# Attention and a two-layer network: the quarter sums of the second weight made by GpSimd from float32 instead of by sign matmuls

## The chip, the cores and the metric

The kernel runs on one core of a Trainium2 chip. The time of a run is the device time of the program in microseconds (us), and lower is better. The engines are named as the profile names them: PE (TensorE, matmuls; PEld are its weight loads), DVE (VectorE), ACT (ScalarE), POOL (GpSimd) and SP (SyncE, which issues most transfers). Each engine takes its instructions in the order in which they were written into its queue, and waits when an operand is not there yet.

## The reference

The input `x` has 8 batches of 8 heads, 512 rows of 64; `state` has 32 rows for each head. Both directions of attention are computed, put together to 544 rows of 512 for each batch, and sent through a normalised network of two layers with ReLU and a residual. The weights are stored in 64-bit floating point.

```python
scale = 1.0 / np.sqrt(D)
scores = scale * np.matmul(x, state.transpose(0, 1, 3, 2))
scores = scores - scores.max(-1, keepdims=True)
a = np.exp(scores)
a /= a.sum(-1, keepdims=True) + 1e-09
xread = np.matmul(a, state)
...
sread = np.matmul(a2, x)
...
xn = (x - mu) / np.sqrt(var + 1e-06) * g_ln
ch = np.maximum(xn @ w_ch1, 0.0) @ w_ch2
return (x + ch).astype(np.float32)
```

`w_ch1` is 512 x 2048 and `w_ch2` 2048 x 512.

## The kernel before

**Precision and tiles.** Every large product is done in float16 halves: a float32 value is split into a high half (`ACTIVATE` with Copy on ACT) and a low half (`SCALAR_TENSOR_TENSOR` on DVE: value times scale, minus the high half), and three matmuls (high x high, high x low, low x high, `TERMS`) replace one. `split` (L663) is that pair. The hidden 2048 columns are worked in four units (`U` = 4) of 512.

**Weights.** `weights1(u)` (L680) and `weights2(u)` (L714) fetch the unit u of the two weights. The 64-bit words land as pairs of 32-bit integers in two landing places (`raws`), each 128 x 2048 words for half of a unit; `words` (L646) builds float32 values out of them, which lie in the first landing place afterwards (`t`). Then come a bound on the size (`sum_of_squares`, `scales`) and the splits into `w1c[u]` and `w2h[u]`. The landing places are parts of buffers that are needed otherwise later (`extra(k)`, whose tile is called `sums`, and `unit(k)`, `narrow(k)`, `wide(k)`, `odd`, called `raw`), so where a unit lands decides from when on it can be fetched and until when it can stay.

**Batch 0** is computed unit by unit while the weights arrive: `state_products` (L750) makes `matrix`, `first_products` (L793) the hidden block with its halves `hid` (the low half of which GpSimd makes, `hid<-strip,hid` 128x512), `second_product` (L813) multiplies with `w2h[u]`, 12 matmuls of 512 columns for each 128 rows (L817); the partial results are added up by transfers that GpSimd issues (`xr<-part`), the last unit's by DVE (`xr<-acc,of_unit,xr`).

**Batches 1 to 7 and the state rows** use Strassen and Winograd's scheme with seven products for the second layer: `products(b)` (L874), with `first` (L901, `half<-ea,matrix`) for the hidden block, `multiply` (L959) for the products and `together` (L968) for the result. A unit of the second weight is seen as four quarters b11, b12, b21, b22 of 128 x 512 values (256 rows by 256 columns), and the scheme needs three or four sums of them besides: b22 - b12, b12 - b11, b22 - b12 + b11, and b21 less the third.

**The sums before** are made by PE from the float16 halves. `sums_of_weights(u)` (L843) multiplies the halves with an identity or its negative (`signs`, L318) and accumulates: 32 matmuls for a unit (L849), 128 in all, each 256 columns; every sum is copied into its high half by ACT (`sums<-acc`, `w2h<-acc`, 128x256) and its low half is made by DVE (`TENSOR_TENSOR sums<-acc,sums`, 128x256), 32 of each in all. The second difference replaces the quarter b12 in `w2h[u]`, so plain second products of batch 0 with that unit have to be done by then; the others lie in `sums16`.

**Attention of batch 1** is made while batch 0 ends. Its softmax in the `ts` layout goes DVE (`dA`, `mA`, `RECIPROCAL mA`), GpSimd (`ts<-ts,mA` 128x1024), DVE (`STREAM_TRANSPOSE ef`), ACT and DVE (`ea`).

**What sets the order.** `PLAN` (L38) is a table written out by hand: items "stream:steps", read in turn by `issue` (L190), which writes each step's instructions into the queues. So the order on each engine is the order of that table, and streams are interleaved as it says. A last stream holds `WARM` (L162) filler matmuls, `half<-ones`, 128x512, whose result nobody reads; they stand between the matmuls of the first 55 us.

Of the kernel before, what the change touches and what calls it, by code (L numbers as in the profile page):

```python
# [9 lines left out]
F16 = mybir.dt.float16  # L10
# [191 lines left out]
def moe_attention(ctx: ExitStack, tc: tile.TileContext, x, state, g_ln, w1, w2, out):  # L202
# [116 lines left out]
    for i in range(2):  # L319
        nc.vector.tensor_scalar(signs[:, i], idf, 1.0 - 2.0 * i, None, ALU.mult)  # L320
# [761 lines left out]
```

## Time and profile before

| | |
|---|---|
| median of 3 runs | 639.22 us (638.99 to 640.02) |
| profiled execution: its own time | 638.32 us |
| its span (first to last instruction) | 636.5 us |
| mean granted TensorE clock | 0.997 |
| ACT, busy | 375.7 us (59%) |
| filler matmuls `half<-ones` | 111, from 1.1 to 54.7 us |
| sign matmuls L849 | 128, from 110.0 to 153.6 us |

The profile's page lists busy time for each engine, the chain of work that ended last, and groups of like instructions. The trace behind it can be asked for a stretch of the span, a line, a tile, or a timeline. In a timeline row the first number is the start in us, the second the length, then engine, line, operation, output `<-` inputs, shape and count; in brackets stands how long the engine had been idle and what ended that. In a row of groups, count, total us and mean ns stand behind the shape, then the idle time before. Rows of instructions that directly follow one another and are alike are drawn together in a timeline, with one length for all of them.

### The profile page before, as it was taken

To read this page: it belongs to the slowest core of one execution; us is meant where nothing else is said; L and a number is where in the kernel's file an instruction comes from. 1 tells how busy PE (TensorE), PEld (TensorE's weight loads), DVE (VectorE), ACT (ScalarE), POOL (GpSimd) and SP (SyncE) were. 2 spreads that over 40 slices of the span, in tenths; PEclk is the share of its full clock that TensorE was granted. 3 is DMA by queue.
4 is the path that set the end of the run, shared out by engine and by line. 5 is a ranking of instruction groups with operands and counts; after the bars stand their busy time and mean duration, and the time that the engine had idled before them with its cause. 6 is when DMAs were issued, how large, how long until landed. Compare 5 with 4: busy or idle time off the path is not lost.

```text
span 636.5 us, 16845 instructions
## 1 busy us (share of the span) xinstructions
PE 621.7 (98%) x7010; PEld 493.6 (78%) x7010; DVE 491.2 (77%) x1105; ACT 375.7 (59%) x686; POOL 228.5 (36%) x189
## 2 busy tenths in 40 slices
PE   9998999999999999999999999999999999999995
PEld 4464555768888888888888888788878888988884
DVE  5999999758795888798778886887487888555543
ACT  5998987768364846584465555755663545343332
POOL 0123435311451335333533453154323544323231
PEclk9999999999999999999999999999999999999998
DMA  8995666330515242515350335043405024201001
GB/s 292 408 267 204 110 158 130 75 79 11 138 34 144 82 77 58 131 26 122 72 150 10 71 91 147 21 78 101 115 2 115 2 44 127 69 1 35 34 34 34
DMA packets 85356, 62.04 MB, mean 97 GB/s; under 512 B 64608, under 2 KB 77408, under 8 KB 84832
## 3 DMA queue, kind: packets, MB, share of 16 engines
q1 hardware_dynamic: 83008, 57.00, 33.4%
q0 software_dynamic: 864, 3.15, 2.7%
q8 instruction: 55, 0.90, 0.6%
q10 hardware_dynamic: 1408, 0.82, 0.4%
q14 instruction: 21, 0.17, 0.1%
HBM read 28.05 MB, written 9.44 MB: 59 GB/s over the span
## 4 chain that ended last, share of the span: by engine, by line
PE 82%; ACT 6%; DVE 6%; DMA 3%; issue 1%; POOL 1%; SPq 0%; ACTq 0%; POOLq 0%; DVEq 0%
PE acc L959 41%; PE half L901 22%; PE half L911 3%; PE banks L757 3%; PE acc L817 3%; PE acc L849 2%; ACT sums L187 1%; DVE raw L187 1%; PE half L187 1%; ACT raw L187 1%; PE banks L594 1%; PE acc L803 1%; PE banks L476 1%; DMA ek<-ek 1%; DMA xr<-part 1%
## 5 line engine op out<-in xcount | busy, mean ns | idle before, releaser
L959 PEld LDWEIGHTS <-xs 128*128 128x128 f16 x2520 | 243.7, 98 | 37.6 <-issue 7.7
L187 POOL TENSOR_TENSOR xs<-rs,xs 128x512 f16<-128x512 f32 x120 | 145.4, 1221 | 270.0 <-ACT xs L187 187.9
L959 PE MATMUL acc<-w2h,xs 128*128 128x256 f16 x1440 | 181.7, 273 | 0.0
L901 PE MATMUL half<-ea,matrix 128*128 128x256 f16 x1344 | 160.8, 273 | 0.1
L901 PEld LDWEIGHTS <-matrix 128*128 128x128 f16 x1344 | 129.9, 98 | 19.6 <-issue 3.0
L959 PE MATMUL acc<-sums,xs 128*128 128x256 f16 x1080 | 140.1, 273 | 0.0
L187 DVE SCALAR_TENSOR_TENSOR rs<-half,rs 128x256 f32<-128x256 f32 x224 | 90.2, 418 | 48.1 <-ACT rs L187 26.7
L187 ACT ACTIVATE xs<-rs 128x512 f16<-128x512 f32 (+1 forms) x128 | 77.2, 618 | 48.6 <-DVE rs L187 46.1
L187 ACT ACTIVATE xs<-half 128x256 f16<-128x256 f32 (+1 forms) x112 | 54.0, 486 | 81.7 <-PE half L901 39.8
L187 DVE SCALAR_TENSOR_TENSOR xs<-half,xs 128x256 f16<-128x256 f32 (+1 forms) x112 | 60.6, 550 | 18.8 <-ACT xs L187 16.3
L187 POOL TENSOR_TENSOR ts<-ts,mA 128x1024 f32<-128x1024 f32 (+1 forms) x16 | 31.6, 1974 | 62.0 <-DVE mA L187 55.5
L187 ACT ACTIVATE rs<-half 128x256 f32<-128x256 f32 x56 | 21.3, 380 | 39.6 <-PE half L901 36.6
L187 DVE SCALAR_TENSOR_TENSOR matrix<-banks,hs,matrix 128x1024 f16<-128x1024 f32 x28 | 35.8, 1279 | 11.2 <-ACT matrix L187 11.0
L817 PE MATMUL acc<-w2h,hid 128*128 128x512 f16 x192 | 43.4, 379 | 0.5 <-DVE of_weights L187 0.5
L187 DVE TENSOR_TENSOR strip<-acc,strip 128x256 f32<-128x256 f32 (+1 forms) x60 | 32.9, 549 | 13.4 <-PE acc L959 10.5
L187 ACT ACTIVATE matrix<-banks,hs 128x1024 f16<-128x1024 f32 x28 | 31.0, 1108 | 12.9 <-PE banks L757 12.7
L187 POOL TENSOR_TENSOR hid<-strip,hid 128x512 f16<-128x512 f32 x16 | 25.4, 1600 | 30.0 <-ACT hid L187 29.5
L817 PEld LDWEIGHTS <-hid 128*128 128x128 f16 x192 | 18.2, 98 | 21.6 <-issue 1.5
L187 PE MATMUL half<-ones 128*128 128x512 bf16 x111 | 27.8, 397 | 1.1 <-DVE ones L316 1.1
L187 DVE SCALAR_TENSOR_TENSOR xr<-strip,of_second,xr 128x512 f32<-128x512 f32 x28 | 26.6, 957 | 0.0
L187 DVE SCALAR_TENSOR_TENSOR x<-x_f,x_s,x 128x512 f16<-128x512 f32 x32 | 24.5, 801 | 1.2 <-ACT x L187 1.0
L187 ACT ACTIVATE x<-x_f,x_s 128x512 f16<-128x512 f32 x32 | 22.0, 713 | 4.8 <-DVE x_s L327 4.6
(156 smaller groups left out, 751.1 us busy)
## 6 DMA issues: line engine op xcount, KB each, us to landing
raw<-in_moe_w_ch_dram SPq DMA_DIRECT2D x10, 1024.0 KB, 8.8
out_dram<-xr SPq DMA_DIRECT2D x16, 512.0 KB, 3.0
x_f<-in_x_dram SPq DMA_DIRECT2D x14, 512.0 KB, 5.3
sums<-in_moe_w_ch_dram SPq DMA_DIRECT2D x6, 1024.0 KB, 7.6
ek<-ea SPq DMA_DIRECT2D x56, 64.0 KB, 2.0
ek<-ek SPq DMA_DIRECT2D x7, 512.0 KB, 4.3
xr<-part POOLq DMA_DIRECT2D x6, 512.0 KB, 5.4
s_r<-in_state_dram SPq DMA_DIRECT2D x28, 64.0 KB, 3.5
```

The lines of the kernel that those rows point to most:

```text
L187: return lambda: f(*map(now, args), **{k: now(v) for k, v in kw.items()})
L476: nc.tensor.matmul(o[32 * j:32 * j + 32], lhsT=state_of(b, sT, g, j, a), rhs=xT[:, 2 * j + g].rearrange("p c t -> p (c t)"), start=a == 0, ...
L594: nc.tensor.matmul(px[:, c, D * h:D * h + D], lhsT=ek[:, h % 2, h // 2, (2 * t + c) * P:(2 * t + c + 1) * P], rhs=sk[:, h], start=True, st ...
L757: nc.tensor.matmul(ps[g][32 * j:32 * j + 32], lhsT=state_of(b, sT, g, j, i)[r], rhs=w[r, k, j], start=n == 0, stop=n == 2, skip_group_chec ...
L803: nc.tensor.matmul(o[:, 256 * f:256 * f + 256], lhsT=m[:, g, i, P * (q + f):P * (q + f) + P], rhs=ea[:, s, k, g], start=f == 0 and g == 0 ...
L817: nc.tensor.matmul(po, lhsT=hid[:, i, q, c * P:(c + 1) * P], rhs=w[:, j, q], start=first and q == 0 and n == 0, stop=last and q == 3 and n ...
L849: nc.tensor.matmul(o, lhsT=signs[:, k // 2], rhs=v[k], start=start and k == 0, stop=k == 3, skip_group_check=True)
L901: nc.tensor.matmul(ps[:, 256 * q:256 * q + 256], lhsT=m[:, h, i, P * (2 * k + q):P * (2 * k + q) + P], rhs=ea[:, 0, j, h, 256 * g:256 * g ...
L911: nc.tensor.matmul(ps[:, 256 * q:256 * q + 256].rearrange("p (t n) -> p t n", t=2), lhsT=w[:, i, j, fs], rhs=xsT[:, :, x, j], start=q == 0 ...
L959: nc.tensor.matmul(po[o], lhsT=y[:, n, i, o] if o < 2 else x[:, o - 2, n, i], rhs=v[j], start=u == 0 and n == 0 and k == 0 and o in (2, 1, ...
```

## The change

The sums are made before the split and not after it. When the float32 values of a unit of the second weight have been split into `w2h[u]`, GpSimd takes differences of their quarters in place in the landing place (`w2f[u]`), four `TENSOR_TENSOR` of 128x512 float32 for a unit, 16 in all; then each of the four results is split, as any weight is, by one ACT and one DVE instruction of 128x512: 16 of each. `signs` and the 128 matmuls, 32 copies and 32 subtractions are gone. The results of the splits stay in parts of the `extra` buffers that are free then (`strassen_homes`). As the values of a unit must stay until the sums are made, the last unit of the first weight lands in `unit(2)` and the last of the second in `unit(3)`. `WARM` goes from 111 to 131. The streams of the sums for units 0, 1 and 2 come directly behind unit 2's, so that the numbers of the streams in the table change, and the table is a new one throughout.

```diff
-WARM = 111
+WARM = 131
...
-    signs = main.tile([P, 2, P], F16, name="signs")
-    for i in range(2):
-        nc.vector.tensor_scalar(signs[:, i], idf, 1.0 - 2.0 * i, None, ALU.mult)
...
         raws = ((extra(0), extra(1)), (narrow(2, "raw"), wide(2, "raw")), (extra(1), odd("raw")),
-                (extra(2), odd("raw")))[u]
+                (unit(2, "raw"), odd("raw")))[u]
...
         raws = ((extra(2), odd("raw")), (narrow(3, "raw"), wide(3, "raw")), (extra(0), wide(3, "raw")),
-                (unit(2, "raw"), odd("raw")))[u]
-        t = raws[0]
+                (unit(3, "raw"), odd("raw")))[u]
+        t = w2f[u] = raws[0]
...
-    sums16 = sums.bitcast(F16).rearrange("p (u k i n e) -> p u k i n e", u=U, k=3, i=2, n=2)
+    def quarters(t):
+        v = t.rearrange("p (k n e) -> p k n e", k=2, n=2)
+        return [[v[:, k, :, 256 * i:256 * i + 256] for i in range(2)] for k in range(2)]
+
+    def strassen_homes():
+        (a21, a22), (a11, a12) = quarters(extra(2))
+        (c21, c22), (c11, c12) = quarters(extra(0))
+        e = [extra(1)[:, 512 * k:512 * k + 512].rearrange("p (n e) -> p n e", n=2) for k in range(4)]
+        return [[v.bitcast(F16).rearrange("p n (i e) -> p n i e", i=2) for v in vs]
+                for vs in ((a12, a22, a11), (e[0], e[1], e[2]), (c12, c22, c11), (e[3], a21, c21))]
+    sums16 = strassen_homes()
 
     def sums_of_weights(u):
 
-        w = w2h[u].rearrange("p i (k n) e -> p i n k e", n=2)
...
-                yield do(subtract_all, *[v for d, a, b, p in todo for v in (p, *a, *b)])
-                for d, a, b, p in todo:
-                    yield do(nc.scalar.activation, d[0], p, AF.Copy)
-                    yield do(nc.vector.tensor_tensor, d[1], p, d[0], ALU.subtract)
+
+        (b21, b22), (b11, b12) = quarters(w2f[u])
+        s = of_weights[:, U + u, 0:1]
+        w = w2h[u].rearrange("p i (k n) e -> p n i k e", n=2)[:, :, :, 1, 256:512]
+        DIFF = nc.gpsimd.tensor_tensor
+        yield do(DIFF, b22, b22, b12, ALU.subtract)
+        yield do(DIFF, b12, b12, b11, ALU.subtract)
+        yield do(DIFF, b11, b22, b11, ALU.add)
+        yield do(DIFF, b21, b21, b11, ALU.subtract)
+        for o, v in ((w, b12), (sums16[u][0], b22), (sums16[u][1], b11), (sums16[u][2], b21)):
+            yield from split(o[:, :, 0], o[:, :, 1], v, s)
...
-    streams += [common_scale(), attention(1), state_products(1), *map(sums_of_weights, range(U))]
+        if u == 2:
+            streams += map(sums_of_weights, (0, 1, 2))
+    streams += [common_scale(), attention(1), state_products(1), sums_of_weights(3)]
```

Where instructions stand now is seen in the engines' queues. First, seven of the 16 new splits on DVE stand among the last weights of batch 0. This is a piece of DVE's new queue (`sums<-sums,of_weights`, `sums<-raw,of_weights,sums` and `w2h<-...` with 128x2x256 are the new splits; those of 128x1024 split the weights themselves):

```order
L185 SCALAR_TENSOR_TENSOR w2h<-sums,of_weights,w2h 128x2x256
...
L185 SCALAR_TENSOR_TENSOR sums<-sums,of_weights 128x2x256
L185 SCALAR_TENSOR_TENSOR sums<-sums,gx,acc 128x512 x4
L185 SCALAR_TENSOR_TENSOR w1c<-sums,of_weights,w1c 128x1024 x2
L185 SCALAR_TENSOR_TENSOR w2h<-sums,of_weights,w2h 128x1024
L185 TENSOR_REDUCE mB<-banks 128x2
L321 TENSOR_SCALAR mB<-mB,es 128x1 x2
L185 SCALAR_TENSOR_TENSOR matrix<-acc,matrix 128x512 x2
L185 SCALAR_TENSOR_TENSOR sums<-raw,of_weights,sums 128x2x256 x3
L185 SCALAR_TENSOR_TENSOR w2h<-raw,of_weights,w2h 128x2x256
L185 SCALAR_TENSOR_TENSOR sums<-sums,of_weights 128x2x256
```

All seven stand ahead of the next place, DVE's queue around batch 1's RECIPROCAL, which releases `ts` on GpSimd. Before:

```order
L187 RECIPROCAL mA<-mA 128x32
L187 TENSOR_TENSOR w2h<-acc,w2h 128x256
L187 TENSOR_TENSOR sums<-acc,sums 128x256
L187 STREAM_TRANSPOSE ef<-ts 128x1024
L187 TENSOR_TENSOR w2h<-acc,w2h 128x256
L327 TENSOR_SCALAR of_unit<-rf_1087,uoq 128x1 x4
L187 SCALAR_TENSOR_TENSOR ea<-ef,ea 128x1024
L187 TENSOR_TENSOR w2h<-acc,w2h 128x256 x2
L187 SCALAR_TENSOR_TENSOR matrix<-banks,hs,matrix 128x2x512
```

and now:

```order
L185 RECIPROCAL mA<-mA 128x32
L185 TENSOR_SCALAR ux<-x_i 128x1
L321 TENSOR_SCALAR hs<-uoq,r 128x1 x4
L185 TENSOR_SCALAR of_second<-uo 128x1
L185 STREAM_TRANSPOSE ef<-ts 128x1024
L185 SCALAR_TENSOR_TENSOR matrix<-banks,hs,matrix 128x2x512
L185 SCALAR_TENSOR_TENSOR ea<-ef,ea 128x1024
L185 SCALAR_TENSOR_TENSOR w2h<-sums,of_weights,w2h 128x2x256
L185 SCALAR_TENSOR_TENSOR sums<-sums,of_weights 128x2x256
L185 SCALAR_TENSOR_TENSOR matrix<-banks,hs,matrix 128x2x512
```

The subtractions between `RECIPROCAL` and `matrix` are gone; `hs` has moved to behind the RECIPROCAL, and `of_unit` to ahead of it; new splits follow `ea`.

The third place is GpSimd's queue from the hidden lows of unit 2 (the first `hid` x4) to the first hidden block of batch 1 (`xs<-rs,xs`). Before:

```order
L187 TENSOR_TENSOR hid<-strip,hid 128x2x256 x4
L187 DMA xr<-part 128x1024
L187 TENSOR_TENSOR ts<-ts,mA 128x1024
L187 DMA xr<-part 128x1024
L187 TENSOR_TENSOR ts<-ts,mA 128x1024
L187 TENSOR_TENSOR hid<-strip,hid 128x2x256 x4
L187 TENSOR_TENSOR xs<-rs,xs 128x4x128 x5
```

and now, the differences being `sums<-sums` and `raw<-raw`:

```order
L185 TENSOR_TENSOR hid<-strip,hid 128x2x256 x4
L185 DMA xr<-part 128x1024
L185 TENSOR_TENSOR sums<-sums 128x2x256
L185 TENSOR_TENSOR ts<-ts,mA 128x1024
L185 DMA xr<-part 128x1024
L185 TENSOR_TENSOR raw<-raw 128x2x256
L185 TENSOR_TENSOR ts<-ts,mA 128x1024
L185 TENSOR_TENSOR hid<-strip,hid 128x2x256 x2
L185 TENSOR_TENSOR sums<-sums 128x2x256
L185 TENSOR_TENSOR hid<-strip,hid 128x2x256 x2
L185 TENSOR_TENSOR raw<-raw 128x2x256 x2
L185 TENSOR_TENSOR xs<-rs,xs 128x4x128
```

Twelve of the 16 differences stand ahead of the last unit's `hid` (two of them are shown here, ten further up), and four behind. On PE, the first hidden block of batch 1 (24 matmuls of `first`) now stands behind 12 matmuls of the last unit's second product, 24 state products and 12 more of the second product, counted from that unit's first second product on; before, one block of 12 second products stood there. Behind it stand no sign matmuls (88 before), 24 second products of batch 0 (36 before) and 24 state products fewer than before.

More of the change, by code (lines that the diff above doesn't have):

```diff
@@ L637, in statistics @@
         yield columns(len(rows_of), rf, rs, isst, SB, ALU.mult, ALU.mult)
-    w1c, w2h = [None] * U, [None] * U
+    w1c, w2h, w2f = [None] * U, [None] * U, [None] * U
     is1 = Later(lambda: tiny("is1", U))
@@ L839, in second_products_by_unit @@
                 yield from store_batch(0, t)
-    sums16 = sums.bitcast(F16).rearrange("p (u k i n e) -> p u k i n e", u=U, k=3, i=2, n=2)
-    def sums_of_weights(u):
-        w = w2h[u].rearrange("p i (k n) e -> p i n k e", n=2)
-        def subtract(start, o, *v):
-            for k in range(4):
-                nc.tensor.matmul(o, lhsT=signs[:, k // 2], rhs=v[k], start=start and k == 0, stop=k == 3,
-                                 skip_group_check=True)
-        for n in range(2):
-            ps = [accumulator() for _ in range(2)]
-            (b21, b22), (b11, b12) = ([[w[:, i, n, k, 256 * x:256 * x + 256] for i in range(2)] for x in range(2)]
-                                      for k in range(2))
-            t3, t2, n4 = ([sums16[:, u, k, i, n] for i in range(2)] for k in range(3))
-            o = [v[:, 256 * x:256 * x + 256] for v in ps for x in range(2)]
-            for pairs in (((t3, b22, b12), (b12, b12, b11)), ((t2, b22, b12),), ((n4, b21, t2),)):
-                first = len(o)
-                def subtract_all(*v, first=first):
-                    for k in range(len(v) // 5):
-                        subtract(first != 1 and k == 0, *v[5 * k:5 * k + 5])
-                todo = [(d, a, b, o.pop(0)) for d, a, b in pairs]
-                yield do(subtract_all, *[v for d, a, b, p in todo for v in (p, *a, *b)])
-                for d, a, b, p in todo:
-                    yield do(nc.scalar.activation, d[0], p, AF.Copy)
-                    yield do(nc.vector.tensor_tensor, d[1], p, d[0], ALU.subtract)
@@ L956, in multiply @@
                                 q, e = ((n, 0), None, (n + 2, 0), None, None, (n + 2, 256), (n, 256))[o] or (None, None)
-                                v = [w[:, j, q, e:e + 256] if q is not None else wt[:, {3: 0, 4: 1, 1: 2}[o], j, n] for j in range(2)]
+                                v = [w[:, j, q, e:e + 256] if q is not None else wt[{3: 0, 4: 1, 1: 2}[o]][:, n, j] for j in range(2)]
                                 for k, (i, j) in enumerate(TERMS):
@@ L962, in strassen_products @@
                     for ops in ((2, 0, 1), (4,), (3, 5), (6,)):
-                        yield do(lambda po, *a, ops=ops: multiply(ops, [v() for v in po], *a), po, x, y, w2h[u], sums16[:, u])
+                        yield do(lambda po, *a, ops=ops: multiply(ops, [v() for v in po], *a), po, x, y, w2h[u], sums16[u])
                 yield strassen_hidden()
```

242 rows, old and new, of the table PLAN are left out of this document.

## The prediction

> **What bounds the kernel now.** I began with the page's header and its first part, which say which engine is full, and then cut the span into stretches, because a share of the whole span hides where another engine rules.
>
> ```profile
> span 636.5 us, 16845 instructions
> PE 621.7 (98%) x7010; PEld 493.6 (78%) x7010; DVE 491.2 (77%) x1105; ACT 375.7 (59%) x686; POOL 228.5 (36%) x189
> ```
>
> PE is 98% busy over the span. The stretches divide that (start:end, length, then busy time of each engine):
>
> ```profile
> 10.00:58.50 48.50, 43.78 (x608) 24.21 (x606) 47.51 (x90) 46.58 (x73) 11.96 (x7) 1.00 0.89 319
> 58.50:113.00 54.50, 53.84 (x528) 30.10 (x528) 52.88 (x122) 46.13 (x67) 21.30 (x16) 1.00 0.61 135
> 113.00:123.50 10.50, 10.27 (x84) 7.92 (x82) 8.10 (x18) 9.14 (x20) 5.55 (x5) 1.00 0.38 77
> 123.50:300.00 176.50, 176.50 (x2031) 145.80 (x2030) 140.58 (x318) 104.57 (x211) 62.49 (x52) 1.00 0.35 84
> ```
>
> From 10 to 113 us both PE and DVE look full: DVE works 47.51 of 48.5 us and 52.88 of 54.5. Part of PE's busy time there is filler (`WARM`), so fewer matmuls would end nothing sooner in these 103 us; DVE's list does. From 123.5 us on PE has no idle time at all and DVE has a fifth of its time free. So the kernel has two parts: up to the first hidden block of batch 1 (call its start S) DVE and what hangs on it set the pace, and behind S PE does. S and PE's price of one matmul are in PE's timeline:
>
> ```profile
> 119.16 1.91 PE L849 MATMUL acc<-w2h,signs 128*128 128x256 f16 x16 [0.23 <-DVE w2h L187]
> 120.90 2.75 PE L817 MATMUL acc<-w2h,hid 128*128 128x512 f16 x12
> 123.49 1.47 PE L901 MATMUL half<-ea,matrix 128*128 128x256 f16 x12
> ...
> 127.08 0.84 PE L757 MATMUL banks<-w1c,sT 64*32 64x512 f16 x24
> 127.85 0.39 PE L849 MATMUL acc<-w2h,signs 128*128 128x256 f16 x2
> ```
>
> S is 123.49. Durations of matmuls overlap, so a price is taken from one start to the next: 16 sign matmuls in 120.90 - 119.16 = 1.74 us are 0.109 each; 12 second products (L817) in 2.59 are 0.216 each; 24 state products (L757) take 127.85 - 127.08 = 0.77.
>
> **Behind S: what PE saves.** The groups of PE in the stretch from 123.45 to the end:
>
> ```profile
> L757 PE MATMUL banks<-w1c,sT 64*32 64x512 f16 x648 | 22.7, 379 | 0.5 <-DVE matrix L187 0.5
> L849 PE MATMUL acc<-w2h,signs 128*128 128x256 f16 x72 | 10.2, 273 | 0.0
> L817 PE MATMUL acc<-w2h,hid 128*128 128x512 f16 x37 | 8.6, 379 | 0.0
> L849 PE MATMUL acc<-sums,signs 128*128 128x256 f16 x16 | 3.1, 273 | 0.0
> ```
>
> 88 of the 128 sign matmuls stand behind S, and 36 whole second products (the 37th row is one that straddles the cut). In the changed order no sign matmul is left, 24 second products stand behind S, and of the state products one set of 24 has moved ahead of S. PE's work behind S shrinks by 88 x 0.109 + 12 x 0.216 + 0.77 = 9.6 + 2.6 + 0.8 = 13.0 us. PE is full there, so all of it counts: 636.5 - 123.5 = 513.0 us become 500.0. Also gone behind S are the subtractions of the sums on DVE and the copies on ACT; neither engine bounds there, so I price them at nothing; 16 new splits of 128x512 on each take their place, 9 of them behind batch 1's RECIPROCAL (below), and what covers those is the hidden blocks that PE does first. **The span afterwards is S + 500.0**, and the question is where S goes: 13.0 us is the gain if it stays.
>
> **Ahead of S: what DVE gets.** Seven of the 16 new splits stand on DVE ahead of batch 1's RECIPROCAL, which starts the chain to S. Their price is that of a split of the same shape, `x<-x_f,x_s,x`; less the 0.04 us by which one instruction starts ahead of the other's end, 0.70 each.
>
> ```profile
> L187 DVE SCALAR_TENSOR_TENSOR x<-x_f,x_s,x 128x512 f16<-128x512 f32 x8 | 5.8, 742 | 0.0
> ...
> L327 DVE TENSOR_SCALAR hs<-uoq,r 128x1 f32<-128x1 f32 x4 | 0.6, 205 | 0.0
> L327 DVE TENSOR_SCALAR hr<-uoq,r 128x1 f32<-128x1 f32 x4 | 0.6, 204 | 0.0
> ```
>
> ```profile
> 115.11 0.34 DVE L187 RECIPROCAL mA<-mA 128x32 f32<-128x32 f32 x1
> ...
> 117.55 1.25 DVE L187 STREAM_TRANSPOSE ef<-ts 128x1024 f32<-128x1024 f32 x1 [1.49 <-POOL ts L187]
> ...
> 119.03 0.56 DVE L327 TENSOR_SCALAR of_unit<-rf,uoq 128x1 f32<-128x1 f32 x4
> ...
> 122.13 1.28 DVE L187 SCALAR_TENSOR_TENSOR matrix<-banks,hs,matrix 128x1024 f16<-128x1024 f32 x1
> ```
>
> That is +4.9 us. `hs` and `hr`, four each, move behind the RECIPROCAL (-1.2), one set of `of_unit` moves ahead of it (+0.6), one old subtraction is gone (-0.4); the word and split instructions keep their number, their other landing places being worth some 0.0 (I take nothing). Net **+3.9 us**. The old kernel's two sign scalings cost nothing either way: DVE waits for the first input then.
>
> ```profile
> 6.66 0.69 DVE L187 TENSOR_REDUCE most<-x_f 128x1 f32<-128x512 f32 x1 [4.96 <-DMA x_f<-in_x_dram]
> ```
>
> **GpSimd's differences, and what they do to DVE.** Sixteen are added, 128x512 float32 of two inputs, 12 of them ahead of the last unit's hidden lows. The trace has none of the kind. The 128x256 ones (`strip<-strip`) take 0.73, the 128x1024 ones 1.90; the nearest row is `hid`, of the same count of elements, 1.15 when alone. GpSimd is busy a third of the time, so I price its own time at nothing except at the end of the chain. What they do to DVE is the unknown. In the first 113 us some DVE instructions are longer than their like, each under a GpSimd instruction:
>
> ```profile
> L187 POOL TENSOR_TENSOR hid<-strip,hid 128x512 f16<-128x512 f32 x12 | 20.8, 1748 | 21.3 <-ACT hid L187 20.7 <-issue 0.5
> ```
>
> ```profile
> 40.41 2.18 POOL L187 TENSOR_TENSOR hid<-strip,hid 128x512 f16<-128x512 f32 x1 [2.80 <-ACT hid L187]
> 47.36 1.55 POOL L187 TENSOR_TENSOR hid<-strip,hid 128x512 f16<-128x512 f32 x1 [4.78 <-ACT hid L187]
> 53.51 4.30 POOL L187 TENSOR_TENSOR hid<-strip,hid 128x512 f16<-128x512 f32 x2 [4.60 <-ACT hid L187]
> ```
>
> ```profile
> 41.46 1.67 DVE L187 SCALAR_TENSOR_TENSOR ea<-ef,ea 128x512 f16<-128x512 f32 x1
> ...
> 47.94 2.06 DVE L187 SCALAR_TENSOR_TENSOR raw<-raw 128x1024 uint32<-128x1024 uint32 x1
> 49.92 1.27 DVE L187 SCALAR_TENSOR_TENSOR w2h<-sums,of_weights,w2h 128x1024 f16<-128x1024 f32 x1
> ...
> 53.47 1.22 DVE L187 SCALAR_TENSOR_TENSOR sums<-sums 128x1024 uint32<-128x1024 uint32 x1
> 54.72 2.07 DVE L187 SCALAR_TENSOR_TENSOR sums<-raw 128x1024 uint32<-128x1024 uint32 x1
> ...
> 95.63 1.88 DVE L187 SCALAR_TENSOR_TENSOR w2h<-sums,of_weights,w2h 128x1024 f16<-128x1024 f32 x1
> ```
>
> `ea` took 1.67 against 0.74 for a split of its size, two word instructions 2.06 and 2.07 against 1.22, one `w2h` split 1.88 against 1.27: 0.93 + 0.84 + 0.85 + 0.61 = 3.2 us. Twelve `hid` and three `ts` ran on GpSimd in these 103 us, so one of them cost DVE 3.2 / 15 = 0.22 us on average. GpSimd paid too: 1.75 us for a `hid` instead of 1.15. The two ends for 12 new instructions are 0 (none meets a DVE instruction that minds) and 12 x 0.8 = 9.8 us (each stretches one as the four were stretched). I take the average, 12 x 0.22 = **+2.6 us**, since the new instructions fall among the same kind of DVE work.
>
> One rule speaks against the change. The Trainium skill says in "SBUF — State Buffer", section "Who interferes with whom", that DVE's second port pair is also GpSimd's only one, that it is an exclusive lock for whichever came first, and that nothing else among the engines' ports contends. The stretched rows above agree with it in kind, but only 4 of 15 GpSimd instructions cost DVE anything. By the rule at its hardest, with every new difference holding DVE for a `hid`'s 1.15 us, the cost would be 13.8 us in place of 2.6 and the time, as an estimate, about 645.
>
> **The chain to S.** The old chain, with GpSimd's rows beside those of DVE above:
>
> ```profile
> 115.61 1.90 POOL L187 TENSOR_TENSOR ts<-ts,mA 128x1024 f32<-128x1024 f32 x1 [2.12 <-DVE mA L187]
> 117.49 1.15 POOL L187 TENSOR_TENSOR hid<-strip,hid 128x512 f16<-128x512 f32 x1
> ```
>
> The RECIPROCAL ends at 115.45; `ts` runs on GpSimd to 117.51 and the last unit's first `hid` behind it to 118.64. In the old order only one L817 block stood between there and S, and `matrix` (to 123.41) ended last. In the new one GpSimd has the same queue, `ts`, then `hid`, but PE has two second-product blocks of the last unit and a set of state products between that `hid` and S. New RECIPROCAL: 115.45 + 3.9 + 2.6 = 122.0; `ts` 122.1 to 124.0; `hid` to 125.2; PE 0.1 later, then 2 x 2.59 + 0.77 = 5.95: **S = 131.3**. Beside it, DVE's own way (`ef` 1.25, `matrix` 1.28, `ea` 1.28 behind `ts`) ends at 124.0 + 3.8 = 127.8, covered. The 20 more fillers (20 x 0.216 = 4.3 us) stand ahead of the first second product, where PE waits for DVE's splits; nothing is priced for them.
>
> **Sum.** Span 131.3 + 500.0 = 631.3. The profiled run took 638.32, 1.82 beyond its span, so 633.1; the median shown, 639.22, is 0.90 above the profiled run, so the forecast on its footing is **634.0 us**, 0.8% below. A difference of 0.2% (1.3 us) is about what a measurement here can tell from none.
>
> **Rivals.**
> - *The early idle time is used* (0.24). DVE waits some 5 us for its first inputs, and from 113 to 123.5 it is idle 2.4 us, mostly behind `ts`. Work moved into these holes hides the 3.9 us of splits, perhaps part of the stretches. For it: the whole order is new. Against it: the first hole waits for a transfer, which no order fills. S is then 126.5 to 129, the time 629 to 632.
> - *DVE loses nothing* (0.05): S stays near 123.5 to 125 and PE's 13 us come through: 626 to 627.5.
> - *The gain is eaten* (0.09): the time lands within 0.2%, 638 to 640.5, which takes an S of 135.3 to 137.8, 4 to 6.5 us more delay than I summed, as when half of the new differences hit DVE.
> - *GpSimd holds up DVE each time* (0.16), slower. The place is DVE's list from 10 us to the RECIPROCAL, nearly full in both stretches and made of two-input splits and word instructions; the price is the 0.8 us that each of the four stretched rows shows, for 12 differences 9.8 us in place of 2.6. S is then 138.5, the span 638.5, the time 641.2. It decides from 2.6 + 6.5 = 9.1 us on, 0.76 us for each difference. Against it: 11 of 15 GpSimd instructions cost DVE nothing. The lock that the Trainium skill tells of ("SBUF — State Buffer", "Who interferes with whom") would be this mechanism.
>
> **How the numbers follow.** The forecast's case, 632 to 638, holds 0.46 (the range is that of 0.1 to 0.5 us of stretch for a difference, and some early idle time used). Taking the first, third and fourth rivals in, the range is 627 to 641.5, leaving the second rival's edge and the hardest form of the last outside. Faster by over 0.2%: 0.46 + 0.24 + 0.05 = 0.75; within: 0.09; slower: 0.16.
>
> **What would show it.** In the changed kernel the first hidden block should start near 131, and the rest of the span should be 500; if the rest is longer, PE waits behind S, and the first `multiply` is the place. DVE's RECIPROCAL of batch 1 near 122, `ts` right behind, the last unit's first `hid` at 124 and PE idle or filling before it. Between 10 and 113 us DVE's two-input instructions should show some 6 us of stretch instead of 3.2; 12 or more would mean the last rival. The forecast is wrong if the new splits land in idle time, or if PE comes late behind S for want of splits of the sums.

## The result, and the profile after

The changed kernel takes **645.63 us** (median of 4 runs, 644.49 to 646.43) against 639.21 before (four runs): 1.0097 of its time, 95% interval 1.0078 to 1.0115. It is 1% slower; the forecast was 634.0, and the range, 627 to 641.5, does not hold it. The page of the changed kernel begins

```profile
span 644.7 us, 16600 instructions
PE 619.6 (96%) x6902; PEld 485.3 (75%) x6902; DVE 503.7 (78%) x1087; ACT 377.8 (59%) x670; POOL 246.4 (38%) x205
```

PE is busy for 2.1 us less, 619.6 for 621.7, and yet the span is 8.2 us longer. The same stretches as before (engines in the same order; the number behind the counts is the granted clock):

```profile
10.00:58.50 48.50, 43.83 (x586) 23.85 (x585) 47.62 (x81) 48.05 (x70) 7.65 (x6) 1.00 0.92 320
58.50:113.00 54.50, 46.42 (x326) 24.68 (x325) 49.24 (x107) 35.70 (x57) 27.12 (x21) 0.87 0.48 116
```

Up to 58.5 us PE and DVE are as busy as before. From 58.5 to 113 DVE is idle for 5.3 us of 54.5 (1.6 before) and PE for 8.1 (0.7 before), and PE's granted clock fell to 0.87. The chain that the prediction followed, in DVE's, GpSimd's and PE's timelines:

```profile
134.14 0.35 DVE L185 RECIPROCAL mA<-mA 128x32 f32<-128x32 f32 x1
```

```profile
134.64 1.91 POOL L185 TENSOR_TENSOR ts<-ts,mA 128x1024 f32<-128x1024 f32 x1 [0.50 <-DVE hs L321]
136.51 2.27 POOL L185 TENSOR_TENSOR hid<-strip,hid 128x512 f16<-128x512 f32 x2
```

```profile
143.36 2.78 PE L893 MATMUL half<-ea,matrix 128*128 128x256 f16 x24
```

The chain has the shape that was forecast, but it starts 19.0 us later than before (115.45 to 134.49) where 6.5 were summed. S is 143.36, and 644.7 - 143.4 = 501.3 us follow.

Where the 19.0 us are: I took the usual length of each operation and shape on DVE and added up what instructions ahead of the RECIPROCAL took beyond it (over 0.15 us each). The work at usual lengths is 3.1 us more than before, the stretch 14.1 us instead of 3.6, the idle time 13.8 us instead of 9.4; the last 1.0 us is smaller overlap between instructions. Most of the stretched rows, in DVE's timeline:

```profile
56.86 2.11 DVE L185 SCALAR_TENSOR_TENSOR sums<-raw 128x1024 uint32<-128x1024 uint32 x1
58.90 2.17 DVE L185 SCALAR_TENSOR_TENSOR sums<-sums 128x1024 uint32<-128x1024 uint32 x1
...
65.70 2.10 DVE L185 SCALAR_TENSOR_TENSOR sums<-raw 128x1024 uint32<-128x1024 uint32 x1
...
73.47 1.76 DVE L185 SCALAR_TENSOR_TENSOR x<-x_f,x_s,x 128x512 f16<-128x512 f32 x1
...
80.81 1.42 DVE L185 TENSOR_SCALAR raw<-raw 128x1024 uint32<-128x1024 uint32 x1
82.34 2.10 DVE L185 SCALAR_TENSOR_TENSOR sums<-raw 128x1024 uint32<-128x1024 uint32 x1
...
85.10 1.83 DVE L185 SCALAR_TENSOR_TENSOR sh<-s_j,x_s,sh 128x128 f16<-128x128 f32 x1
...
94.57 3.89 DVE L185 SCALAR_TENSOR_TENSOR sums<-sums,of_weights 128x512 f16<-128x512 f32 x1
...
123.76 3.01 DVE L185 SCALAR_TENSOR_TENSOR w1c<-raw,of_weights,w1c 128x1024 f16<-128x1024 f32 x1
```

Usual are 1.22, 1.22, 1.22, 0.74, 0.69, 1.22, 0.34, 0.74 and 1.27. Each of these rows lies beside GpSimd instructions. GpSimd beside the three that lost most:

```profile
83.30 1.05 POOL L185 DMA_DIRECT2D xr<-part  x1
84.09 1.57 POOL L185 TENSOR_TENSOR sums<-sums 128x512 f32<-128x512 f32 x1
85.54 1.24 POOL L185 TENSOR_TENSOR hid<-strip,hid 128x512 f16<-128x512 f32 x1
...
93.40 0.88 POOL L185 DMA_DIRECT2D xr<-part  x1 [6.62 <-ACT part L185]
94.01 1.45 POOL L185 TENSOR_TENSOR hid<-strip,hid 128x512 f16<-128x512 f32 x1
95.13 1.55 POOL L185 TENSOR_TENSOR raw<-raw 128x512 f32<-128x512 f32 x1
96.35 1.55 POOL L185 TENSOR_TENSOR sums<-sums 128x512 f32<-128x512 f32 x1
...
123.48 0.88 POOL L185 DMA_DIRECT2D xr<-part  x1 [0.22 <-issue]
124.10 1.57 POOL L185 TENSOR_TENSOR sums<-sums 128x512 f32<-128x512 f32 x1
```

The split that begins at 94.57 ends 0.56 us after the last of three GpSimd instructions; alone it takes 0.74, so nearly all of its work came behind them. The idle time has rows of its own in the waits of DVE; behind them stand PE's timeline and a piece of the chain that ended last:

```profile
DVE w2h L185 <- ACT w2h L185: 2.8, 2, 2.6
DVE sums L185 <- ACT sums L185: 1.2, 1, 1.2
```

```profile
84.50 1.03 PE L668 MATMUL acc<-sums 128*128 128x128 bf16 x8 [2.15 <-DVE sums L185]
85.47 1.94 PE L696 MATMUL acc<-sums,gm 128*32 128x512 f32 x8
87.34 0.19 PE L349 MATMUL acc<-of_columns,ones 128*128 128x1 bf16 x1
87.38 6.90 PE L811 MATMUL acc<-w2h,hid 128*128 128x512 f16 x24
```

```profile
87.52 4.19 PE acc L811 x12
91.80 0.73 ACT w2h L185
92.55 0.75 DVE w2h L185
```

PE waits for the late DVE and then runs slowly (granted clock 0.50 from 85 to 90 us): 24 second products take 6.9 us where two of the blocks of before, one behind the other, would take 5.3 (2.59 + 2.75). The first 12 of them take 4.19 us in place of 2.59. ACT's split into `w2h` may not overwrite the quarter before those 12 have read it, and DVE waits for ACT.

### The profile page after: what moved, and what is told of

The parts are those of the page before. It is cut to its first block, busy times and chain, and to the rows that moved or that the text cites. A ratio compares the mean times of both kernels' runs of the same rounds, so it can differ in the third digit from the quotient of the medians.

```text
span 644.7 us, 16600 instructions
## 1 busy us (share of the span) xinstructions
PE 619.6 (96%) x6902; PEld 485.3 (75%) x6902; DVE 503.7 (78%) x1087; ACT 377.8 (59%) x670; POOL 246.4 (38%) x205
## 4 chain that ended last, share of the span: by engine, by line
PE 76%; DVE 19%; ACT 3%; issue 1%; DVEq 0%; ACTq 0%
PE acc L951 41%; PE half L893 22%; DVE sums L185 4%; PE half L903 3%; PE banks L751 3%; DVE raw L185 3%; PE acc L811 2%; DVE w1c L185 2%; PE half L185 1%; DVE w2h L185 1%; PE banks L563 1%; PE banks L588 1%; PE banks L470 1%; DVE xs L185 1%; DVE x L185 1%
## 5 line engine op out<-in xcount | busy, mean ns | idle before, releaser
L185 POOL TENSOR_TENSOR xs<-rs,xs 128x512 f16<-128x512 f32 x120 | 143.9, 1211 | 253.8 <-ACT xs L185 169.8
L951 PE MATMUL acc<-sums,xs 128*128 128x256 f16 x1080 | 142.2, 273 | 0.0
L185 ACT ACTIVATE xs<-rs 128x512 f16<-128x512 f32 x128 | 77.1, 618 | 69.3 <-DVE rs L185 62.5
L185 POOL TENSOR_TENSOR ts<-ts,mA 128x1024 f32<-128x1024 f32 (+1 forms) x16 | 30.1, 1880 | 65.2 <-DVE mA L185 62.9
L811 PE MATMUL acc<-w2h,hid 128*128 128x512 f16 x192 | 46.7, 399 | 0.1
L185 DVE SCALAR_TENSOR_TENSOR matrix<-banks,hs,matrix 128x1024 f16<-128x1024 f32 x28 | 35.8, 1279 | 11.9 <-ACT matrix L185 11.9
L185 ACT ACTIVATE matrix<-banks,hs 128x1024 f16<-128x1024 f32 x28 | 31.1, 1111 | 11.8 <-PE banks L751 11.8
L185 PE MATMUL half<-ones 128*128 128x512 bf16 x131 | 33.1, 398 | 1.1 <-DVE part_mean L356 1.1
L185 POOL TENSOR_TENSOR hid<-strip,hid 128x512 f16<-128x512 f32 x16 | 23.6, 1483 | 13.2 <-ACT hid L185 13.2
L185 DVE BATCH_NORM_STATS2 s<-xr 128x6 f32<-128x512 f32 x32 | 21.8, 685 | 5.3 <-ACT xr L185 5.3
```

The costliest lines, as they stand in the source:

```text
L185: return lambda: f(*map(now, args), **{k: now(v) for k, v in kw.items()})
L811: nc.tensor.matmul(po, lhsT=hid[:, i, q, c * P:(c + 1) * P], rhs=w[:, j, q], start=first and q == 0 and n == 0, stop=last and q == 3 and n ...
L951: nc.tensor.matmul(po[o], lhsT=y[:, n, i, o] if o < 2 else x[:, o - 2, n, i], rhs=v[j], start=u == 0 and n == 0 and k == 0 and o in (2, 1, ...
```

## The experiments

"RECIPROCAL" is its end, S the start of the first hidden block, "stretch" and "idle" as above. Ratios are to the kernel before, run beside it; its medians on these six occasions were 639.1 to 639.8 us, so a difference of less than about 1 us between runs of different occasions is not read. The last four columns come from one execution each, and DVE's idle time in the first 20 us alone, ahead of every difference, is 7.0 to 8.6 us in them.

| run | median us | ratio (95%) | RECIPROCAL | S | stretch | idle |
|---|---|---|---|---|---|---|
| before | 639.21 | 1 | 115.5 | 123.5 | 3.6 | 9.4 |
| the change | 645.63 | 1.0097 (1.0078 to 1.0115) | 134.5 | 143.4 | 14.1 | 13.8 |
| 1 tiny differences | 633.51 | 0.9896 (0.9845 to 0.9947) | 122.6 | 131.5 | 5.2 | 10.8 |
| 2 on DVE | 643.71 | 1.0073 (1.0046 to 1.0100) | 130.3 | 139.8 | 6.6 | 9.8 |
| 3 fillers | 644.04 | 1.0081 (1.0051 to 1.0111) | 132.3 | 141.2 | 14.2 | 11.6 |
| 4 unit 0 late | 644.92 | 1.0084 (1.0038 to 1.0129) | 132.5 | 142.8 | 8.4 | 16.9 |
| 5 twice | 647.86 | 1.0132 (1.0103 to 1.0161) | 134.2 | 143.9 | 15.7 | 12.2 |
| 6 halves | 637.56 | 0.9980 (0.9968 to 0.9991) | 127.2 | 136.1 | 10.4 | 10.3 |
| 7 tiny, fillers | 636.23 | 0.9948 (0.9925 to 0.9970) | 125.2 | 134.1 | 5.2 | 13.1 |
| 8 by transfer | 653.61 | 1.0222 (1.0166 to 1.0278) | 140.5 | 149.8 | 6.0 | 27.3 |
| 9 halves, lows too | 640.77 | 1.0020 (1.0002 to 1.0038) | 130.3 | 139.0 | 13.0 | 10.9 |
| 10 quarters | 638.45 | 0.9991 (0.9977 to 1.0005) | 128.9 | 137.8 | 10.3 | 12.1 |
| 11 before, lows in halves | 637.74 | 0.9978 (0.9963 to 0.9994) | 114.4 | 122.4 | 2.3 | 9.4 |
| 12 halves, 111 fillers | 640.38 | 1.0010 (0.9993 to 1.0026) | 129.5 | 138.3 | 9.8 | 12.9 |
| 13 one transfer behind | 644.60 | 1.0082 (1.0057 to 1.0107) | 131.7 | 140.5 | 13.2 | 11.8 |
| 14 same, halves | 637.49 | 0.9974 (0.9961 to 0.9987) | 127.1 | 136.0 | 10.2 | 10.3 |
| 15 both behind | 641.97 | 1.0033 (1.0021 to 1.0044) | 129.5 | 138.3 | 11.4 | 11.6 |
| 16 both behind, halves | **635.77** | 0.9957 (0.9937 to 0.9976) | 125.1 | 133.9 | 7.4 | 11.1 |

**1, tiny differences.**

```diff
-        yield do(DIFF, b22, b22, b12, ALU.subtract)
+        t = lambda v: v[:, :, 0:1]
+        yield do(DIFF, t(b22), t(b22), t(b12), ALU.subtract)
...
```

> The changed kernel, but each of the 16 differences on GpSimd takes only the first column of each half (128x2 instead of 128x512): all their waits and places stay, most of the differences are left out. Port theory (a GpSimd instruction with its operands in SBUF holds up DVE's two-input instructions, which cost the changed kernel 10.5 us of stretch more than before): the stretch ahead of batch 1's RECIPROCAL falls from 14.1 us to 5 or less, the RECIPROCAL comes near 125 instead of 134, the time is 634 to 637. Wait theory (the changed kernel is late because splits in place wait for second products, and PE runs these at a lower granted clock after it had idled): DVE's waits of 2.6 and 1.2 us stay and the time is 642 or more.

The time fell by 12.1 us. The RECIPROCAL ends at 122.6 where the prediction had put it at 122.0, S is 131.5 (131.3 in the prediction), and 500.1 us follow. Order, landing places and splits are the same, so the failure lies in GpSimd's arithmetic. Of the 11.9 us at the RECIPROCAL 8.9 are stretch and 3.0 idle time, so most of the new waits followed from it. That GpSimd itself was late, a rival which this run leaves open, is ruled out by run 5 below.

**2, on DVE.** `DIFF = nc.vector.tensor_tensor`.

> The changed kernel with the 16 differences on DVE instead of GpSimd, nothing else moved. Port theory: DVE takes 12 x 0.67 = 8 us more of its own ahead of the RECIPROCAL and loses some 8 to 10 us of stretch, so the time is about that of the changed kernel, 643 to 646. Wait theory, with no price for the port: DVE only gets more to do, and the time is 651 or more.

As the port theory had it: with 8.1 us more work of its own DVE is still 4.2 us earlier.

**3, fillers.** In the table of the order, `177:131-138` ahead of step `12:8`, `177:139-148` ahead of `12:9`, `177:149-154` ahead of `13:0`, and `WARM = 155`.

> The changed kernel with 24 more filler matmuls (5.2 us of PE work), 8 and 10 ahead of the two halves of the bound of unit 2's first weight (where PE idled 1.6 and 2.2 us), 6 ahead of unit 2's state products (1.1 us). Wait theory: the granted clock stays at 1.0 from 80 to 110 us, the first-weight means and second products that took 1.87 and 4.19 us take 1.1 and 2.6, DVE's waits of 2.6 and 1.2 us go, and the time falls by 3 to 4 us to 641 to 643. Port theory: DVE's stretch stays at 14 us and the time changes by less than 1.5 us.

Between the two: the granted clock is 1.00 from 58.5 to 113 us, the idle time falls by 2.2 and S by 2.2, the time by 1.6; the stretch stays. Behind the first 20 us DVE's idle time falls from 6.2 us to 3.2, as far as in run 1, so the slow clock is a second loss, the smaller one. What it is worth in time is less sure: the intervals of the two ratios overlap.

**4, unit 0 late.** Steps `17:4` to `17:9` moved to stand ahead of `17:10`.

> The changed kernel with three of unit 0's four splits of sums (of b12, b22 and the third sum) moved from DVE's list before batch 1's RECIPROCAL to behind it, next to the fourth. The differences on GpSimd stay where they are. Wait theory: 2 or 3 splits (1.4 to 2.1 us) and the wait of 2.6 us leave the list, the RECIPROCAL comes 4 to 5 us earlier, the time is 641 to 642. Port theory: only the splits go, and what GpSimd's three instructions in a row did to the second of them (3.9 instead of 0.7 us) hits the next DVE instruction instead; the time is 643 to 645.

The stretch fell by 5.7 us, 3.2 of them with the 3.9 us split, but the idle time grew by 3.1 and the chain behind the RECIPROCAL by 1.4: the time is within 1 us of the change. The hold did not pass to the next DVE instruction, which the port theory had said it would; DVE was waiting when GpSimd's row ran.

**5, twice.** Each `DIFF` issues its instruction two times.

> The changed kernel with each of the 16 differences issued twice in a row on GpSimd (the sums then hold a quarter taken off twice). Port theory: the price goes with GpSimd's busy time, so 12 more instructions of 128x512 ahead of batch 1's RECIPROCAL cost about as much again as the first 12 (11.9 us between tiny and full differences): stretch 20 to 24 us, RECIPROCAL 142 to 147, time 653 to 659. If instead only a few collisions by chance of this order cost so much: time within 4 us of the changed kernel, up to 650.

A miss: 2.2 us for 16 more instructions, and the RECIPROCAL is no later. The price does not go with GpSimd's busy time. Most DVE instructions that met a pair lost what was left of its first instruction, and the second was held in its turn: the pair at 56.47 took 4.26 us, where one instruction alone takes 1.26. The hold that cost most, in a split of 2.60 us, lasted through two.

**6, halves.**

```diff
-        DIFF = nc.gpsimd.tensor_tensor
+        def DIFF(o, a, b, op):
+            for k in range(2):
+                nc.gpsimd.tensor_tensor(o[:, k], a[:, k], b[:, k], op)
```

> The changed kernel with each difference as two GpSimd instructions of 128x256 (0.73 us each by the row of that shape, against 1.15 to 1.3 for the whole). If DVE can come in between two GpSimd instructions, a held-up DVE instruction waits for half as long and the stretch falls from 14 to 10 us or less, the time to 641 to 643. If GpSimd holds DVE for its whole busy time, back to back, the longer total (12 x 0.25 = 3 us more) makes it the same or up to 3 us slower: 645 to 649.

8.1 us less than the change, and 0.2% below the kernel before. Of the 7.3 us at the RECIPROCAL 3.7 are stretch and 3.5 idle time. Three of the rows shown above, in this kernel:

```profile
57.42 1.56 DVE L185 SCALAR_TENSOR_TENSOR sums<-raw 128x1024 uint32<-128x1024 uint32 x1
58.91 1.75 DVE L185 SCALAR_TENSOR_TENSOR sums<-sums 128x1024 uint32<-128x1024 uint32 x1
...
90.28 3.88 DVE L185 SCALAR_TENSOR_TENSOR sums<-sums,of_weights 128x512 f16<-128x512 f32 x1
```

The hold went from 0.89 to 0.34 us in the first: it waits for the end of one GpSimd instruction, now a shorter one. The last stayed: it ends 0.56 us behind a row of five, as it did behind three.

**7, tiny differences and fillers.**

> The differences cut to one column as in the first experiment, and the 24 fillers of the third: what is left of the waits when GpSimd's work is gone. If the waits behind a lower granted clock are a loss of their own, the time falls by another 1.5 us from 633.5 to 632. If they only followed from the late DVE, PE does not idle at those places now and the fillers change less than 0.7 us, or cost up to 2 us.

2.7 us slower than run 1, more than either theory had. With DVE in time the 24 fillers (5.2 us) stand in PE's way, and DVE's idle time grows by 2.3 us.

**8, by transfer.** Two quarters are negated by ACT; the four differences are `nc.gpsimd.dma_start(out=o, in_=v, accum_op=ALU.add)`.

> The changed kernel with the differences made by transfers that add in place (issued by GpSimd as the partial results are), two quarters of a unit being negated by ACT first (8 instructions of 0.62 us) and split with the negative scale. Port theory: GpSimd reads no operands then, so DVE's stretch falls to about 5 us as with tiny differences; if the transfers land within 4 us each and ACT carries its 5 us, the time is 634 to 640. If issuing them on GpSimd (0.9 us each by the rows of the partial results) or waiting for them holds up the hidden lows behind them in GpSimd's queue, the time is 641 to 650.

The stretch fell as forecast, to 6.0 us, but the idle time doubled: transfers of 256 KB land after 4.2 and 4.8 us in the median and hang on one another, and ACT once waits 10.9 us for one. The time lies above both ranges. (The values that this kernel makes are not those of the change, and why stays open; it shows what such transfers cost, and no more.)

**9 to 12, more pieces.** In 9 `hidden`'s low half on GpSimd is issued in two halves as well, in 11 the same alone in the kernel before; 10 has differences of 128x128; 12 is run 6 less the last 20 fillers.

> The differences in halves as in the sixth experiment, and the 16 hidden lows of batch 0 on GpSimd (128x512, 1.15 us alone) in halves too. Theory of the hold (a DVE instruction that meets one of GpSimd waits until that one instruction ends): the lows held DVE as the differences did (0.6 to 1 us each at three or four places), shorter ones cost half; the time falls by 1 to 2 us more, from 637.6 to 635.5 to 636.5. Against it: more instructions, 16 x 0.25 = 4 us more busy time on GpSimd, some of it on the chain to the first hidden block; no gain or up to 2 us slower.

> Each difference as four GpSimd instructions of 128x128. By the hold of one instruction the stretch of a DVE instruction under a difference falls again, from 0.35 to 0.2 us (it was 0.9 with whole ones), so the time is 636.5 to 637.5 as long as GpSimd keeps up; if the fixed cost of an instruction (0.7 us for two columns) makes a quarter nearly as long as a half, GpSimd has some 10 us more to do, its queue comes late and the time is 639 to 645.

> The kernel before with only its 16 hidden lows in halves. Its four stretched DVE instructions cost 3.2 us; by the hold of one instruction that falls to 1.5 us and the time by 1 to 2 us, to 637.5 to 638.5. If the hold is no matter of an instruction's length: no change within 0.7 us.

> The differences in halves, and the 20 fillers taken out that the change added (the last 20, which stand ahead of the first second product). If they are hidden under PE's waits, the time stays at 637.6 within 0.7 us. If they keep the granted clock up, it falls below 1.0 between 60 and 80 us and the time grows by 1 us or more. If they lie on the path, the time falls by 1 to 4 us.

Run 11 came out as the one-instruction hold has it: stretch from 3.6 to 2.3, 1.4 us faster. Run 9 did not, and is slower than both theories had it: two `w2h` splits took 3.80 and 4.72 us, each through four to six GpSimd instructions. Run 10 won nothing over halves: one split took 4.61 us, through nine GpSimd instructions. In run 12 the granted clock was 0.63 from 58.5 to 70 us and the time grew by 2.8 us; with the 20 fillers (run 6) the clock was 1.00. The 20 fillers keep PE's clock up while it waits for DVE.

**13 to 16, the transfers.** The holds of over 3 us had begun behind GpSimd's issue of a partial result's transfer (`xr<-part`). In 13 and 14 step `6:5`, one such transfer, moves to behind `19:0`; in 15 and 16 also `6:10`, the other of that stretch, to behind `18:3`.

> The changed kernel with one GpSimd transfer (unit 0's first partial result) moved behind the hidden low and the two differences that followed it; nothing else. In the changed kernel GpSimd waited 6.6 us for ACT at this transfer, then ran the three back to back, and the DVE split beside them took 3.9 instead of 0.7 us. Queue theory (the long hold comes from the pile-up behind the waiting transfer): the three run one by one some 6 us earlier, the split takes 1.6 us or less, and the time falls by 2 to 3 us to 642.5 to 643.5. If the split is long for another reason (its own operands, other traffic), it stays at 3.9 us and the time within 1 us of the changed kernel.

> Differences in halves and the same transfer moved behind. Queue theory: the 3.9 us split falls to 1.2 us or less here too and the time falls by 2 to 3 us below the halves alone, to 634.5 to 636. If the transfer, which now lands later, holds up ACT's next partial results, the gain is lost: 637 to 639.

Two misses. In run 13 another instruction, of 0.34 us, took its place, beside four GpSimd instructions in a row behind the transfer that had not been moved:

```profile
85.61 4.15 DVE L185 SCALAR_TENSOR_TENSOR sh<-s_j,x_s,sh 128x128 f16<-128x128 f32 x1
```

```profile
83.82 1.05 POOL L185 DMA_DIRECT2D xr<-part  x1
84.61 1.57 POOL L185 TENSOR_TENSOR sums<-sums 128x512 f32<-128x512 f32 x1
86.05 2.35 POOL L185 TENSOR_TENSOR hid<-strip,hid 128x512 f16<-128x512 f32 x2
88.28 1.33 POOL L185 TENSOR_TENSOR raw<-raw 128x512 f32<-128x512 f32 x1
```

In run 14 an `sh` took 4.27 us, and nothing was won over run 6.

> The changed kernel with both transfers of unit 0's partial results moved behind the differences and hidden lows of that stretch. Issue theory (only behind the issue of a transfer does GpSimd keep DVE out for several instructions): between 80 and 92 us no DVE instruction is held for longer than the GpSimd instruction it met, so the split of 3.9 to 4.2 us takes 2.0 us or less, the RECIPROCAL comes 2 us or more earlier than in the run with one transfer moved (131.5), the time is 640.5 to 642.5. Row theory (any row of GpSimd instructions without a gap): one DVE instruction between 80 and 92 us still takes 3 us or more, time 643.5 to 645.5.

> Differences in halves and both transfers moved behind. Issue theory: the split of 4.2 us falls to 1.2 us or less and the time to 634 to 636. Row theory, or if the later landing of the transfers holds up ACT's next partial results: 637 to 639.

With both moved the row of GpSimd instructions is as long, and the same `sh` comes out short (run 15):

```profile
81.92 3.92 POOL L185 TENSOR_TENSOR sums<-sums 128x512 f32<-128x512 f32 x2
85.80 2.32 POOL L185 TENSOR_TENSOR hid<-strip,hid 128x512 f16<-128x512 f32 x2
88.08 1.27 POOL L185 TENSOR_TENSOR raw<-raw 128x512 f32<-128x512 f32 x1
```

```profile
85.37 0.62 DVE L185 SCALAR_TENSOR_TENSOR sh<-s_j,x_s,sh 128x128 f16<-128x128 f32 x1
88.33 1.16 DVE L185 SCALAR_TENSOR_TENSOR sh<-s_j,x_s,sh 128x128 f16<-128x128 f32 x1
...
118.72 3.02 DVE L185 SCALAR_TENSOR_TENSOR w1c<-raw,of_weights,w1c 128x1024 f16<-128x1024 f32 x1
```

So a row of GpSimd instructions is not enough; here it took the transfer ahead of it. The rows show one more difference: behind the transfer of run 13 each GpSimd instruction begins before the one ahead has ended (84.61 + 1.57 = 86.18, the next at 86.05), by 0.12 to 0.34 us wherever in the changed kernel and in runs 3 to 6 and 9 to 16 a DVE instruction was held through several; in run 15 it is 0.04 us (85.80 + 2.32 = 88.12, the next at 88.08). Whether this overlap keeps DVE out, or only goes with it, no run shows. The last line, behind a transfer left in place (issued at 118.46), is long as ever. Run 16 beats both kernels: 635.77 us, 0.4% below before and 1.5% below the change, with all 16 differences on GpSimd. Its 12 executions form two groups, eight of 635.4 to 636.0 us and four of 639.2 to 639.5.

## Why the prediction was wrong, point by point

- **Behind S.** Forecast 500.0 us, measured 501.3, and 500.1 once GpSimd's work was gone (run 1). Right; the 13.0 us are real. That PE has no idle time from 123.5 us on is more than the row shows, which ends at 300: from there on PE idles for 8.1 us, before and after alike, which left the difference as it was.
- **Seven splits and the moved scalings on DVE, +3.9.** Measured +3.1 at usual lengths. Right.
- **The chain from the RECIPROCAL to S.** Forecast 9.3 us, measured 8.9. Right in size. But PE was to idle or fill ahead of the last unit's first `hid`, and in the changed kernel it has no idle time of over 0.05 us from 126.8 us to S: the chain and PE's own work came out together.
- **GpSimd's differences, +2.6 us of stretch.** Measured +10.5. This is the step that failed: the prediction took the average over 15 instructions of the trace, 0.22 us each, "since the new instructions fall among the same kind of DVE work". In that average stand 11 that were taken to cost DVE nothing; some were held themselves, a `hid` taking 1.75 us on average and 1.15 alone. In the changed kernel 8 of the 12 differences met a DVE instruction. Four held one by 0.9 to 1.1 us each; the other four stand in the three holds behind a transfer, of 1.5, 3.2 and 1.7 us beyond the usual. These seven rows make 10.1 us; the rows beside hidden lows alone make 3.7, as much as before the change. So both the share of meetings and the price of one were too low, and holds through several instructions were not in the sum at all.
- **DVE's idle time, taken as unchanged.** +4.4 us, 0.7 of them in the first 20 us, ahead of every difference. The rest: late DVE lets PE idle, the granted clock falls, second products take longer, and the split in place into `w2h` waits for them. This is the new wait that the prediction had not priced. Run 1 shows 3.0 us of it gone with the stretch; in run 3 fillers take away as much.
- **The fillers, priced at nothing.** Run 12: without the 20 new ones 2.8 us slower (with halves); run 7: with 24 more 2.7 us slower (with tiny differences). They had a price both ways, which I had not worked out.
- **The rivals.** "GpSimd holds up DVE each time", with a chance of 0.16, comes nearest: its 9.8 us against 10.5 measured. That the number is so near is partly luck, since 4 of the 12 differences cost nothing and four stood in longer holds. Its sign, 12 us of stretch between 10 and 113 us, was not quite reached (10.9; 14.1 up to the RECIPROCAL). Its 641.2 fell short mostly by the 4.4 us of idle time.
- **The rule of the Trainium skill** ("SBUF — State Buffer", "Who interferes with whom"). Its lock for a whole instruction is what runs 6 and 11 show: halving the instruction took the hold from 0.89 to 0.34 us. As an estimate of the time, 645, it was nearer than the row's average, by luck: it took 13.8 us of hold, where 10.5 were measured, and none of the idle time. The same section warns that instructions with one input in SBUF can contend as well when they run in a mode that uses both ports; the `TENSOR_SCALAR` of 1.42 us for 0.69 agrees; in which mode it ran no run shows.

## What to carry to other kernels

Work given to GpSimd is not free because GpSimd is idle: price it by what it does to the DVE instructions beside it, with the stretch of those that meet it and not with an average over all. If it must run beside a full DVE, cut it into shorter instructions (8.1 us here) and try to keep the issues of GpSimd's own transfers behind the work that would follow them (3.7 us here with whole differences, 1.8 with halves). A delay of the engine that feeds PE can cost twice: behind waits of 1.6 and 2.2 us PE's granted clock was 0.50 here.

## What the runs showed of the hardware that I had not expected

- Behind GpSimd's issue of a transfer its next instructions can keep a DVE instruction out for several of them in a row: 3.9 us (run of the change), 4.15 (run 13), 4.72 (run 9); in runs 15 and 16 no DVE instruction between 78 and 95 us is more than 0.9 us over its usual length. Not always: in run 6 the `w1c` split beside the transfer at 117.88 took its usual 1.27. There the next two GpSimd instructions overlap by 0.04 us only. What decides it stays open.
- Twice the arithmetic on GpSimd cost 2.2 us more, half the length of an instruction saved 8.1: here the length of one counted, not the sum.
- Quarters of 128x128 gained nothing over halves.
